# The MLP of three batches in 64-row mode, two PSUM tiles at a time with swapped row halves

## The chip, the cores and the metric

The kernel runs on one core of a Trainium2 chip (trn2). The metric is the device time of one execution in microseconds. Each run is repeated, and the runs of two kernels that are compared alternate on the same chip. A profile is of one execution; its span is some 2 us shorter than the device time.

Names used below: PE is the TensorE matmul engine, PEld its weight loads, DVE is VectorE, ACT is ScalarE, POOL is GpSimd. `psc` are scores in PSUM, `est` their exponentials, `pav` the values in PSUM, `pa` and `ph` the two low-rank mixing products, `pt` the first MLP product and `pch` the second. The instructions that empty these PSUM tiles are named by what they write: `xs` (the scaled values, with the 16-bit copy `xh`), `a` (from `pa`), `xf` (`xs` plus `ph`; its transposed copy is `uT`), `tT` (the relu of `pt`) and `of` (the output, from `pch`). `pturn` are transposes of q and k on PE.

## The reference, cut to what matters

```python
# block-sparse attention over 4 batches x 8 heads, 768 x 64 each
scores = scale * np.matmul(q, k.transpose(0, 1, 3, 2))       # masked by 32 x 32 blocks
attn = np.exp(scores - max); attn = attn / attn.sum(-1)
x = np.matmul(attn, v)                                        # -> (4, 768, 512)
# low-rank mixing over the sequence, then an MLP 512 -> 2048 -> 512
h = x.transpose(0, 2, 1) @ U @ V                              # rank 32
u = x + h.transpose(0, 2, 1)
out = u + np.maximum(u @ w_ch1, 0.0) @ w_ch2
```

## The kernel before

Attention works by head pairs (16 in all, four per batch) and by *units*: one exp over a 128x1024 tile of scores, nine units per pair. The MLP of a batch runs as a "fill" between the scores of the next batch. PSUM has eight banks (the Trainium skill, "PSUM — Partial Sum Buffer", Specifications (TRN2)), and the kernel allots them all: four hold two score tiles, and everything else (`pav`, `pa`, `ph`, `pt`, `pch`) shares the other four, chosen by a small clock model at build time. From the second batch on, the scores of each head contract over 64 rows only, so the matmuls of a pair's two heads lie on different row halves and run side by side; the MLP contracts over 128 rows.

```python
    banks = [0.0] * 4                       # when each of the four banks comes free, by the model
    def pst_tile(shape, dtype, name, tag=None):
        if tag is None:
            n = min(range(4), key=lambda n: banks[n])
            clk["pe"] = max(clk["pe"], banks[n])
        ...                                 # cut
    def scores(i, u, est):
        ...                                 # cut
            for h in range(2):              # two matmuls, row halves 0 and 1, two banks
                    mm(o, kT[rows[h], kc], qT[rows[h], q0:q1], True, True)
        keep(nc.scalar.activation(out=est, in_=psc, func=AF.Exp, scale=0.125))

    def mlp_steps(b):
        def w1(jj, c):                      # one pt tile: 4 matmuls of 128 rows x 384 columns
            pt = pst_tile([P, HS], FP32, "pt")
            for cc in range(NCC):
                mm(pt, w1t[:, cc, jj * P : (jj + 1) * P],
                   uT[:, cc, c * HS : (c + 1) * HS], cc == 0, cc == NCC - 1, us=0.162)
            ...                             # relu on ACT or DVE, whichever the model says is first
        def w2(sc, part, n0=0, n1=HD):      # one pch tile: 16 matmuls of 128 rows x 512 columns
            ...                             # cut

    groups = [[x] for x in stream[:SINGLE]]                       # SINGLE = 8
    groups += [stream[n : n + 2] for n in range(SINGLE, len(stream), 2)]
    while gi < len(groups) or work or beside:
        for i, u in groups[gi] if gi < len(groups) else []:
            scores(i, u, est)               # two units per group
        while beside and beside[0][0] <= gi: beside.popleft()[1]()   # second mixing step
        ...                                 # masks on DVE, loads
        if fill: run_fill(sum(c for c, _ in fill) / (to_come[0] - gi))  # MLP steps
        while work and work[0][0] <= gi: work.popleft()[1]()         # values, first mixing step
        gi += 1
```

The softmax here doesn't subtract the row's maximum and nothing guards it: scores larger than these inputs give would overflow.

Of the kernel before, what the change touches and what calls it, by code (L numbers as in the profile page):

```python
# [17 lines left out]
P = 128  # L18
# [3 lines left out]
def kernel(  # L22
# [84 lines left out]
    def pst_tile(shape, dtype, name, tag=None):  # L107
        if tag is None:
            n = min(range(4), key=lambda n: banks[n])
            clk["pe"] = max(clk["pe"], banks[n])  # L110
        else:
            n = pairs[tag][0]
            pairs[tag].rotate(1)
        t = psp.tile(shape, dtype, tag=f"bank{n}", name=name)
        banks[n] = OPEN
        held[id(t)] = (n, t)
        return t
# [8 lines left out]
    def mm(out, lhsT, rhs, start, stop, loose=False, us=0.0):  # L126
        clk["pe"] += us
        keep(
            nc.tensor.matmul(  # L129
                out, lhsT, rhs, start=start, stop=stop, skip_group_check=loose  # L130
            )
        )

# [85 lines left out]
    keep(nc.vector.memset(Vd, 0.0))  # L219
# [138 lines left out]
    mvld = w2t[0:R, 0:3, :].rearrange("r j d -> r (j d)").bitcast(FP32)  # L358
# [123 lines left out]
    def values(i, c, ests, xs, xh):  # L482
        b, hp = divmod(i, HP)
        pav = new_pav()
        for h in range(2):
            for j in range(3):
                for g in range(T):
                    mm(
                        pav[:, j, h, :],
                        weights(ests, g, 3 * c + j, h),  # L490
                        vts[b % 2][:, 2 * hp + h, g, 0 : D + 1],
                        g == 0, g == T - 1, us=0.0315,
                    )
        norm(i, c, pav, xs, xh)

    def mix_a(i, xh, box, part, tag=None):
        if part == 0:
            box["pa"] = pst_tile([P, P], FP32, "pa", tag)
        for sc in range(3 * part, 3 * part + 3):
            mm(box["pa"], Ut[:, sc, :], xh[:, sc, :], sc == 0, sc == T - 1, us=0.056)  # L500
        if part == 1:
            box["a"] = misc.tile([P, P], FP16, tag="a16", name="a16")
            keep(nc.vector.tensor_copy(out=box["a"], in_=box["pa"]))
            give_back(box["pa"], run_on("dve", 0.2))

# [62 lines left out]
    def mlp_steps(b):  # L568
# [3 lines left out]
        def w1(jj, c):  # L572
# [11 lines left out]
            dst = tT[jj][:, c * HS : (c + 1) * HS]  # L584
            ends = {e: max(clk[e], clk["pe"]) + d for e, d in (("act", 0.43), ("dve", 0.48))}
            if ends["act"] <= ends["dve"]:
                keep(nc.scalar.activation(out=dst, in_=pt, func=AF.Relu))  # L587
                give_back(pt, run_on("act", 0.43))
            else:
                keep(nc.vector.tensor_scalar_max(out=dst, in0=pt, scalar1=0.0))  # L590
                give_back(pt, run_on("dve", 0.48))
# [3 lines left out]
        def w2(sc, part, n0=0, n1=HD):  # L595
# [9 lines left out]
            if part == 3:  # L605
                of = opool.tile([P, n1 - n0], FP32, tag="of", name="of")
                keep(
                    nc.vector.tensor_add(out=of, in0=xfs[b][:, sc, n0:n1], in1=pchs[sc])  # L608
                )
                give_back(pchs[sc], run_on("dve", 0.6))  # L610
                keep(
                    nc.sync.dma_start(
                        out=out[b].rearrange("(p t) d -> p t d", t=T)[:, sc, n0:n1],
                        in_=of,
                    )
                )

        for jj in range(NJJ):
            for c in range(2):
                steps.append((0.65, lambda jj=jj, c=c: w1(jj, c)))  # L620
        for sc in range(T):
            cuts = [(0, HD)] if (b, sc) != (B - 1, T - 1) else [(0, 384), (384, HD)]
            for n0, n1 in cuts:
                for part in range(4):
# [3 lines left out]
                            lambda sc=sc, part=part, n0=n0, n1=n1: w2(sc, part, n0, n1),  # L628
                        )
# [46 lines left out]
    def turn_part(i, nm, part):  # L676

        if part == 0:
            turning[nm] = pst_tile([P, T, P], FP16, "pturn", tag="ps")
# [23 lines left out]
    def at_unit(i, u):  # L703
        if (i, u) in MASKS:
            mask_tiles(MASKS.index((i, u)))
        if i == 0:
# [16 lines left out]
            if u == 1:  # L723
# [8 lines left out]
                keep(nc.sync.dma_start(out=mvld, in_=moe_V))  # L732
# [17 lines left out]
        if u == 0:  # L750
            issue(i + 3)
            if i == 1:
                for h in range(2):
                    keep(
                        nc.gpsimd.tensor_copy(
                            out=Ut[:, :, h * D : h * D + R],
                            in_=uld.rearrange("p (t r) -> p t r", t=T),
                        )
                    )
                keep(  # L760
                    nc.gpsimd.tensor_copy(
                        out=Vt[0:R, :, :],
# [3 lines left out]
        if i == 2 and u == 0:  # L766
            for h in range(2):
                keep(nc.sync.dma_start(out=Vd[h * D : h * D + R], in_=Vt[0:R]))
# [29 lines left out]
    def run_fill(us):  # L798
        state["debt"] += us
        while fill and state["debt"] > 0:  # L800
            cost, fn = fill.popleft()
            fn()
            state["debt"] -= cost
# [3 lines left out]
    def pair_tail(i, ests, xs, xh):  # L807
# [3 lines left out]
        def both_a():  # L811
            mix_a(i, xh, box, 0)
            mix_a(i, xh, box, 1)

        def both_h():
# [4 lines left out]
            lambda: values(i, 0, ests, xs, xh),  # L820
            lambda: values(i, 1, ests, xs, xh),
            both_a,
# [5 lines left out]
    groups = [[x] for x in stream[:SINGLE]]  # L828
    groups += [stream[n : n + 2] for n in range(SINGLE, len(stream), 2)]
    LATE = 8  # L830
    OPENS = [5]
    for b in range(1, B):
        last = [n for n, gr in enumerate(groups) if (HP * b + HP - 1, NU - 1) in gr][0]
        OPENS.append(last + 1 + LATE)
# [8 lines left out]
    while gi < len(groups) or work or beside:  # L843
# [13 lines left out]
        for _ in range(len(unmasked) if gi >= SINGLE else 2 if gi > OPENS[0] else 0):  # L857
            i, u, est = unmasked.popleft()
            mask_mul(u, est)
            if u == NU - 1:  # L860
                steps = pair_tail(i, *live.pop(i))
                for at, fn in zip((0, 1, 3), steps):
                    work.append((gi + at, fn))
                beside.append((gi + 5, steps[3]))
# [35 lines left out]
        if fill:  # L900
            to_come = [n for n in OPENS if n > gi] or [gi + 1]
            run_fill(sum(c for c, _ in fill) / (to_come[0] - gi))
# [42 lines left out]
```

## Time and profile before

| | before |
|---|---|
| time, median of the runs | 290.8 us (3 runs), later 290.1 to 290.6 |
| span of the profiled run, clock | 288.9 us, 0.999 |
| PE busy | 279.8 us, 97% |
| prologue, up to the first `pt` matmul | 50.0 us |
| middle, to the start of the last batch's MLP | 194.4 us |
| last batch's MLP, alone, with the closing steps of the program | 44.5 us |

The head of the page of before: span, busy time by engine with its share and instruction count, and PE's row of the 40 equal slices of the span (a digit is the busy share in tenths, 9 is 90% or more).

```profile
span 288.9 us, 6744 instructions
...
PE 279.8 (97%) x2765; PEld 162.0 (56%) x2765; DVE 188.3 (65%) x347; ACT 178.0 (62%) x232; POOL 95.3 (33%) x126
...
PE   7979998899999999999999999999999999999996
```

The chain of work that ended last, by engine and then by line, as shares of the span (the page of before, part 4). L129 is the line of the helper through which nearly all matmuls go, so the names tell them apart:

```profile
PE 84%; DMA 6%; ACT 6%; issue 2%; DVE 1%; POOL 1%; SPq 0%; ACTq 0%; DVEq 0%; POOLq 0%
PE pt L129 29%; PE pch L129 29%; PE psc L129 11%; PE pav L129 10%; ACT est L419 5%; DMA ka<-onehot_const 3%; DMA qld<-in_q_dram 2%; PE pa L129 2%; DMA kld<-in_k_dram 1%; PE ph L129 1%; PE pturn L194 0%; PE puT L563 0%; DVE uT L564 0%; DVE xh L453 0%; DVE m L384 0%
```

And the list of PE's waits of before in the middle, 50 to 244.4 us (who waited for whom, total us, times, longest):

```profile
engine line waited for: us in total, times, longest us
PE pturn L194 <- ACT tT L587: 0.6, 1, 0.6
PE psc L129 <- ACT est L419: 0.5, 1, 0.5
PE pt L129 <- DVE uT L564: 0.2, 1, 0.2
```

PE bounds the middle: it waits 1.3 us in 194. But "busy" is not "at full rate". The Trainium skill says in "Trainium Kernel Development and Optimization", Performance Expectations, that matmul busy time is a bad metric because matmuls are pipelined. It is so here: a 512-column matmul is shown as 380 ns long and the next one starts 216 ns after it. The timeline of PE in before (start, length, form, count):

```profile
137.70 0.49 PE L129 MATMUL pt<-uT,w1t 128*128 128x384 f16 x2
138.12 0.61 PE L129 MATMUL psc<-qT,kT 64*128 64x512 f16 x4
138.66 2.12 PE L129 MATMUL pt<-uT,w1t 128*128 128x384 f16 x12
```

Four score matmuls of 64 rows are two side-by-side pairs of 216 ns, 0.43 us; from 138.12 to 138.66 they take 0.54. The 0.1 us is the change from 64-row to 128-row mode.

**How the ledgers below are made.** From the trace I took the start of every matmul. Two 64-row matmuls of one kind that run side by side count as one. From each start-to-start time I took off the streaming time, as the trace shows it inside long runs (32 ns for 65 columns, 56 for 128, 109 for 256, 162 for 384, 216 for 512). What remains is excess. It is sorted by place: at a change between 64-row and 128-row matmuls 96 ns are booked as mode change; at a swap (known from program order) what is above 40 ns is booked as swap; the rest above 40 ns is booked on what ended just before, and what is below 40 ns is "small". For the middle of before: streaming 180.7 us, mode changes 108 x 96 ns = 10.4 us, waits 2.2 us, small remains 1.0 us; together, but for rounding, the 194.4 us.

### The profile page before, as it was taken

The numbers are of one execution on the slowest core, as the hardware profiler recorded it, in microseconds if no ns is written. First come the engines' busy times: TensorE is split into PE (matmuls) and PEld (weight loads), VectorE is DVE, ScalarE is ACT, GpSimd is POOL, SyncE is SP. The second block draws the span as 40 slices with busy tenths as digits, with TensorE's granted clock in tenths as the row PEclk, the third lists the DMA queues.
The fourth block names the chain that finished last, engine by engine and source line by source line (L and its number), as shares of the span: only waits on it lengthen the run. The fifth ranks groups of instructions, "written<-read, shape, count | busy, mean of one in ns | idle before, by whom it ended". The sixth has DMA issues, their size and how long they took to land.

```text
span 288.9 us, 6744 instructions
## 1 busy us (share of the span) xinstructions
PE 279.8 (97%) x2765; PEld 162.0 (56%) x2765; DVE 188.3 (65%) x347; ACT 178.0 (62%) x232; POOL 95.3 (33%) x126
## 2 busy tenths in 40 slices
PE   7979998899999999999999999999999999999996
PEld 2557775455746454556565545466564644665443
DVE  5756768689997978887886695779787622000112
ACT  3879999687785757577776555577875000776000
POOL 1549853207344454526244261603031201000000
PEclk9999999999999999999999999999999999999999
DMA  5999999962457677773444365161010225000122
GB/s 157 331 261 262 236 254 268 243 169 76 92 140 107 213 160 205 202 153 64 144 108 142 106 173 143 50 93 31 0 31 0 58 80 102 36 0 2 70 75 74
DMA packets 46414, 36.91 MB, mean 128 GB/s; under 512 B 27272, under 2 KB 42896, under 8 KB 46384
## 3 DMA queue, kind: packets, MB, share of 16 engines
q1 hardware_dynamic: 43208, 32.06, 41.6%
q0 software_dynamic: 2688, 4.19, 8.1%
q8 instruction: 21, 0.34, 0.5%
q10 hardware_dynamic: 488, 0.24, 0.3%
q14 instruction: 9, 0.07, 0.1%
HBM read 27.80 MB, written 6.29 MB: 118 GB/s over the span
## 4 chain that ended last, share of the span: by engine, by line
PE 84%; DMA 6%; ACT 6%; issue 2%; DVE 1%; POOL 1%; SPq 0%; ACTq 0%; DVEq 0%; POOLq 0%
PE pt L129 29%; PE pch L129 29%; PE psc L129 11%; PE pav L129 10%; ACT est L419 5%; DMA ka<-onehot_const 3%; DMA qld<-in_q_dram 2%; PE pa L129 2%; DMA kld<-in_k_dram 1%; PE ph L129 1%; PE pturn L194 0%; PE puT L563 0%; DVE uT L564 0%; DVE xh L453 0%; DVE m L384 0%
## 5 line engine op out<-in xcount | busy, mean ns | idle before, releaser
L419 ACT ACTIVATE est<-psc 128x1024 f16<-128x1024 f32 x144 | 138.8, 1023 | 47.4 <-PE psc L129 47.2
L129 PE MATMUL pt<-uT,w1t 128*128 128x384 f16 x512 | 89.1, 327 | 0.2 <-DVE uT L564 0.2
L129 PE MATMUL pch<-w2t,tT 128*128 128x512 f16 (+2 forms) x400 | 87.9, 371 | 0.0
L431 DVE TENSOR_TENSOR est<-est,m 128x1024 f16<-128x1024 f16 x108 | 84.7, 828 | 0.0
L129 PEld LDWEIGHTS <-w1t 128*128 128x128 f16 x512 | 47.6, 98 | 38.2 <-issue 8.4
L587 ACT ACTIVATE tT<-pt 128x384 f16<-128x384 f32 x82 | 39.3, 495 | 36.1 <-PE pt L129 34.9
L129 PEld LDWEIGHTS <-tT 128*128 128x128 f16 x400 | 36.4, 98 | 44.3 <-issue 5.4
L129 PEld LDWEIGHTS <-est 128*128 128x128 f16 x1152 | 44.0, 97 | 10.6 <-issue 0.5
L471 POOL CAST xh<-xs 128x384 f16<-128x384 f32 x30 | 21.4, 716 | 84.7 <-DVE xs L453 82.5
L608 DVE TENSOR_TENSOR of<-xf,pch 128x512 f32<-128x512 f32 (+2 forms) x25 | 16.6, 662 | 49.9 <-PE pch L129 49.8
L129 PE MATMUL pav<-vt,est 128*128 128x65 f16 x1152 | 46.4, 193 | 0.1
L129 PE MATMUL psc<-qT,kT 64*128 64x512 f16 (+1 forms) x288 | 33.9, 327 | 0.9 <-ACT est L419 0.8
L549 POOL CAST uh<-xf 128x384 f16<-128x384 f32 x24 | 16.1, 697 | 38.3 <-issue 33.6
L590 DVE TENSOR_SCALAR tT<-pt 128x384 f16<-128x384 f32 x46 | 24.2, 548 | 0.9 <-PE pt L129 0.7
L129 PE MATMUL psc<-qa,ka 128*128 128x512 f16 (+1 forms) x96 | 21.8, 326 | 1.9 <-DMA ka<-onehot_const 1.5
L448 DVE RECIPROCAL rcp<-pav 128x6 f32<-128x6 f32 x32 | 6.2, 194 | 21.1 <-PE pav L129 20.6
L453 DVE TENSOR_TENSOR xs<-pav,rcp 128x384 f32<-128x384 f32 x32 | 17.8, 557 | 1.9
L188 POOL CAST kst<-kld 128x768 f16<-128x768 f32 x15 | 16.5, 1100 | 5.5 <-PE pt L129 2.0
L188 POOL CAST qst<-qld 128x768 f16<-128x768 f32 x15 | 16.5, 1100 | 3.6 <-PE pa L129 2.5
L129 PEld LDWEIGHTS <-kT 64*128 64x128 f16 x288 | 10.1, 94 | 13.4 <-issue 8.8
L182 POOL CAST vt<-vld 128x768 f16<-128x768 f32 x16 | 15.0, 939 | 5.7 <-DMA vld<-in_v_dram 5.7
L544 DVE TENSOR_TENSOR xf<-xs,ph 128x384 f32<-128x384 f32 x24 | 12.2, 548 | 4.5 <-PE ph L129 4.5
(57 smaller groups left out, 111.5 us busy)
## 6 DMA issues: line engine op xcount, KB each, us to landing
vld<-in_v_dram SPq DMA_DIRECT2D x16, 384.0 KB, 5.0
out_dram<-of SPq DMA_DIRECT2D x23, 256.0 KB, 2.2
qld<-in_q_dram SPq DMA_DIRECT2D x15, 384.0 KB, 4.4
kld<-in_k_dram SPq DMA_DIRECT2D x15, 384.0 KB, 4.1
w1t<-in_moe_w_ch_dram POOLq DMA_DIRECT2D x4, 512.0 KB, 10.2
w2t<-in_moe_w_ch_dram POOLq DMA_DIRECT2D x4, 512.0 KB, 19.5
qld<-in_q_dram SPq DMA_DIRECT2D x1, 256.0 KB, 3.1
kld<-in_k_dram SPq DMA_DIRECT2D x1, 256.0 KB, 4.5
```

The lines of the kernel that those rows point to most:

```text
L129: nc.tensor.matmul(out, lhsT, rhs, start=start, stop=stop, skip_group_check=loose)
L182: nc.gpsimd.tensor_copy(out=vts[b % 2][:, 2 * hp : 2 * hp + 2, :, 0:D], in_=ld)
L188: keep(nc.gpsimd.tensor_copy(out=st.rearrange("p t h d -> p h t d"), in_=ld))
L419: keep(nc.scalar.activation(out=est, in_=psc, func=AF.Exp, scale=0.125))
L431: keep(nc.vector.tensor_tensor(out=o, in0=o, in1=m, op=ALU.mult))
L453: nc.vector.tensor_tensor(out=o.rearrange("p j (h d) -> p j h d", h=2), in0=pav[:, :, :, 0:D], in1=rcp[:, :, :, None].broadcast_to([P, 3, ...
L471: keep(nc.gpsimd.tensor_copy(out=xh[:, 3 * c : 3 * c + 3, :], in_=x3))
L544: nc.vector.tensor_tensor(out=u3, in0=xs[:, tc3, :], in1=phs[c], op=ALU.add)
L549: keep(nc.gpsimd.tensor_copy(out=uh[:, tc3, :], in_=u3))
L587: keep(nc.scalar.activation(out=dst, in_=pt, func=AF.Relu))
L590: keep(nc.vector.tensor_scalar_max(out=dst, in0=pt, scalar1=0.0))
L608: nc.vector.tensor_add(out=of, in0=xfs[b][:, sc, n0:n1], in1=pchs[sc])
```

## The change

The intent is to take away most of the 108 mode changes: if the MLP and the mixing products run in 64-row mode too, they can follow the scores with no drain. Each 128-row matmul becomes two 64-row matmuls on the two row halves. The Trainium skill ("TensorEngine Tiling (Array Packing)", Gotcha 1: PSUM Pressure) says that different row tiles cannot use one PSUM bank at the same time. So two tiles are made at once: in the first half of the work row half 0 adds to tile 0 and row half 1 to tile 1, then they swap. Between the two halves the kernel makes PE wait until its own last matmul has left the array, because the other row half now writes that bank; the scores of one unit are placed there to cover the wait. Values stay in 128-row mode, both halves of a pair in one burst. The last batch, which has no scores to cover swaps, stays in 128-row mode.

The core of the diff (cut; comments are mine):

```diff
+    def half_wait(ins):                       # PE waits for its own earlier matmul
+        nop = nc.tensor.nop(nofuse=True)
+        tc.add_manual_dep(nop.ins, ins.ins.name, ...)
+        keep(nop)
...
-    def values(i, c, ests, xs, xh):
+    def values(i, ests, xs, xh):              # both halves, c = 0 and 1, in one burst
...
+    def mix_a_rows(xh, box):                  # pa in two banks, one per row half, summed on DVE
+        pas = [pst_tile([P, P], FP32, "pa") for r in range(2)]
...
+        def w1_rows(jj, phase):
+            if phase == 0:
+                pair[0] = [pst_tile([P, HS], FP32, "pt") for c in range(2)]
+            pts = pair[0]
+            if phase == 1:
+                half_wait(pair[2])
+            for cc in range(NCC):
+                for r in ((0, 1), (1, 0))[phase]:
+                    c = r ^ phase
+                    last = mm(pts[c], w1t[rows[r], cc, jj * P : (jj + 1) * P],
+                        uT[rows[r], cc, c * HS : (c + 1) * HS],
+                        phase == 0 and cc == 0, phase == 1 and cc == NCC - 1, True, us=0.081)
+            if phase == 0:
+                pair[2] = half_done(last)
+            else:
+                for c in range(2):
+                    relu(tT[jj][:, c * HS : (c + 1) * HS], pts[c])
...                                            # w2_rows likewise, 16 pairs per half
     def run_fill(us):
         state["debt"] += us
+        n = 0
         while fill and state["debt"] > 0:
+            if fill[0][2] and n and us < 1e6:  # a second half waits for the next scores
+                break
...
-    groups = [[x] for x in stream[:SINGLE]]
-    groups += [stream[n : n + 2] for n in range(SINGLE, len(stream), 2)]
+    groups = [[x] for x in stream]            # one unit per group
...
-                for at, fn in zip((0, 1, 3), steps):
-                    work.append((gi + at, fn))
-                beside.append((gi + 5, steps[3]))
+                work.append((gi, steps[0]))
+                work.append((gi + 5, steps[1]))
+                beside.append((gi + 9, steps[2]))
...                                            # in the prologue: V loaded twice (mvld), U copied
-                            out=Ut[:, :, h * D : h * D + R],      # in 4 pieces of 64 rows, not 2
+                                out=Ut[rows[r], :, at : at + R],
```

More of the change, by code (lines that the diff above doesn't have):

```diff
@@ L109, in pst_tile @@
             n = min(range(4), key=lambda n: banks[n])
+            assert banks[n] < OPEN
             clk["pe"] = max(clk["pe"], banks[n])
@@ L127, in mm, with half_done @@
         clk["pe"] += us
-        keep(
-            nc.tensor.matmul(
-                out, lhsT, rhs, start=start, stop=stop, skip_group_check=loose
-            )
-        )
+        ins = nc.tensor.matmul(
+            out, lhsT, rhs, start=start, stop=stop, skip_group_check=loose
+        )
+        keep(ins)
+        return ins
+    def half_done(ins):
+        return ins
+    def half_wait(ins):
+        nop = nc.tensor.nop(nofuse=True)
+        tc.add_manual_dep(
+            nop.ins, ins.ins.name,
+            mybir.DependencyInfo(mybir.DependencyClass.Sync, mybir.DependencyReason.DATA),
+            reason="halves",
+        )
+        keep(nop)
     id16 = consts.tile([P, P], FP16)
@@ L218 @@
     keep(nc.vector.memset(Vt, 0.0))
-    keep(nc.vector.memset(Vd, 0.0))
     qld, kld = new_ld(0, "q"), new_ld(0, "k")
@@ L357 @@
     uld = w2t[:, 3, 0 : 2 * T * R].bitcast(FP32)
-    mvld = w2t[0:R, 0:3, :].rearrange("r j d -> r (j d)").bitcast(FP32)
+    mvld = w2t[0 : 2 * R, 0:3, :].rearrange("r j d -> r (j d)").bitcast(FP32)
     def load_w1(cc):
@@ L480, in new_pav @@
         return pst_tile([P, 3, 2, D + 1], FP32, "pav", tag)
-    def values(i, c, ests, xs, xh):
+    def values(i, ests, xs, xh):
         b, hp = divmod(i, HP)
-        pav = new_pav()
-        for h in range(2):
-            for j in range(3):
-                for g in range(T):
-                    mm(
-                        pav[:, j, h, :],
-                        weights(ests, g, 3 * c + j, h),
-                        vts[b % 2][:, 2 * hp + h, g, 0 : D + 1],
-                        g == 0, g == T - 1, us=0.0315,
-                    )
-        norm(i, c, pav, xs, xh)
+        for c in range(2):
+            pav = new_pav()
+            for h in range(2):
+                for j in range(3):
+                    for g in range(T):
+                        mm(
+                            pav[:, j, h, :],
+                            weights(ests, g, 3 * c + j, h),
+                            vts[b % 2][:, 2 * hp + h, g, 0 : D + 1],
+                            g == 0, g == T - 1, us=0.0315,
+                        )
+            norm(i, c, pav, xs, xh)
     def mix_a(i, xh, box, part, tag=None):
@@ L504, in mix_a @@
             give_back(box["pa"], run_on("dve", 0.2))
+    def mix_a_rows(xh, box):
+        pas = [pst_tile([P, P], FP32, "pa") for r in range(2)]
+        for sc in range(T):
+            for r in range(2):
+                mm(pas[r], Ut[rows[r], sc, :], xh[rows[r], sc, :], sc == 0, sc == T - 1, us=0.027)
+        a16 = box["a"] = misc.tile([P, P], FP16, tag="a16", name="a16")
+        keep(nc.vector.tensor_copy(out=a16, in_=pas[0]))
+        give_back(pas[0], run_on("dve", 0.2))
+        keep(nc.vector.tensor_tensor(out=a16, in0=a16, in1=pas[1], op=ALU.add))
+        give_back(pas[1], run_on("dve", 0.2))
     def mix_h(i, c, a16, xs, uh, tag=None, quick=False):
@@ L583, in w1 @@
                 )
-            dst = tT[jj][:, c * HS : (c + 1) * HS]
-            ends = {e: max(clk[e], clk["pe"]) + d for e, d in (("act", 0.43), ("dve", 0.48))}
-            if ends["act"] <= ends["dve"]:
-                keep(nc.scalar.activation(out=dst, in_=pt, func=AF.Relu))
-                give_back(pt, run_on("act", 0.43))
-            else:
-                keep(nc.vector.tensor_scalar_max(out=dst, in0=pt, scalar1=0.0))
-                give_back(pt, run_on("dve", 0.48))
+            relu(tT[jj][:, c * HS : (c + 1) * HS], pt)
         pchs = {}
@@ L605, in w2 @@
             if part == 3:
-                of = opool.tile([P, n1 - n0], FP32, tag="of", name="of")
-                keep(
-                    nc.vector.tensor_add(out=of, in0=xfs[b][:, sc, n0:n1], in1=pchs[sc])
-                )
-                give_back(pchs[sc], run_on("dve", 0.6))
-                keep(
-                    nc.sync.dma_start(
-                        out=out[b].rearrange("(p t) d -> p t d", t=T)[:, sc, n0:n1],
-                        in_=of,
-                    )
-                )
+                leave(sc, n0, n1, pchs[sc])
@@ new lines, in mlp_steps, with relu @@
+        pair = {}
+        def relu(dst, pt):
+            ends = {e: max(clk[e], clk["pe"]) + d for e, d in (("act", 0.43), ("dve", 0.48))}
+            if ends["act"] <= ends["dve"]:
+                keep(nc.scalar.activation(out=dst, in_=pt, func=AF.Relu))
+                give_back(pt, run_on("act", 0.43))
+            else:
+                keep(nc.vector.tensor_scalar_max(out=dst, in0=pt, scalar1=0.0))
+                give_back(pt, run_on("dve", 0.48))
+        def w1_rows(jj, phase):
+            if phase == 0:
+                tT[jj] = tpool.tile([P, S], FP16, tag="tT", name="tT")
+                pair[0] = [pst_tile([P, HS], FP32, "pt") for c in range(2)]
+            uT = uTs[b].rearrange("p n t s -> p n (t s)")
+            pts = pair[0]
[4 more added lines that the diff above has]
+                    c = r ^ phase
+                    last = mm(
+                        pts[c],
+                        w1t[rows[r], cc, jj * P : (jj + 1) * P],
+                        uT[rows[r], cc, c * HS : (c + 1) * HS],
+                        phase == 0 and cc == 0, phase == 1 and cc == NCC - 1, True,
+                        us=0.081,
+                    )
+            if phase == 0:
+                pair[2] = half_done(last)
+            else:
+                for c in range(2):
+                    relu(tT[jj][:, c * HS : (c + 1) * HS], pts[c])
@@ new lines, in leave, with w2_rows @@
+        def leave(sc, n0, n1, pch):
+            of = opool.tile([P, n1 - n0], FP32, tag="of", name="of")
+            keep(nc.vector.tensor_add(out=of, in0=xfs[b][:, sc, n0:n1], in1=pch))
+            give_back(pch, run_on("dve", 0.6))
+            keep(
+                nc.sync.dma_start(
+                    out=out[b].rearrange("(p t) d -> p t d", t=T)[:, sc, n0:n1],
+                    in_=of,
+                )
+            )
+        def w2_rows(s0, phase, part):
+            if phase == 0 and part == 0:
+                pair[1] = [pst_tile([P, HD], FP32, "pch") for c in range(2)]
+            if phase == 1 and part == 0:
+                half_wait(pair[2])
+            for jj in range(4 * part, 4 * part + 4):
+                for r in ((0, 1), (1, 0))[phase]:
+                    c = r ^ phase
+                    last = mm(
+                        pair[1][c],
+                        tT[jj][rows[r], (s0 + c) * P : (s0 + c + 1) * P],
+                        w2t[rows[r], jj, :],
+                        phase == 0 and jj == 0, phase == 1 and jj == NJJ - 1, True,
+                        us=0.1085,
+                    )
+            if phase == 0 and part == 3:
+                pair[2] = half_done(last)
+            if phase == 1 and part == 3:
+                for c in range(2):
+                    leave(s0 + c, 0, HD, pair[1][c])
@@ new lines, in mlp_steps @@
+        if b < B - 1:
+            for jj in range(NJJ):
+                for phase in range(2):
+                    steps.append((0.65, lambda jj=jj, ph=phase: w1_rows(jj, ph), phase == 1))
+            for s0 in range(0, T, 2):
+                for phase in range(2):
+                    for part in range(4):
+                        steps.append(
+                            (
+                                0.87,
+                                lambda s0=s0, ph=phase, part=part: w2_rows(s0, ph, part),
+                                phase == 1 and part == 0,
+                            )
+                        )
+            return steps
@@ L618, in mlp_steps @@
         for jj in range(NJJ):
             for c in range(2):
-                steps.append((0.65, lambda jj=jj, c=c: w1(jj, c)))
+                steps.append((0.65, lambda jj=jj, c=c: w1(jj, c), False))
         for sc in range(T):
@@ L628, in mlp_steps @@
                             lambda sc=sc, part=part, n0=n0, n1=n1: w2(sc, part, n0, n1),
+                            False,
                         )
@@ L678, in turn_part @@
         if part == 0:
-            turning[nm] = pst_tile([P, T, P], FP16, "pturn", tag="ps")
+            turning[nm] = pst_tile([P, T, P], FP16, "pturn", tag="ps" if i < HP + 1 else None)
         turn_some(sts[i, nm], turning[nm], 3 * part, 3 * part + 3)
@@ L731, in at_unit @@
                 issue(2, "v")
-                keep(nc.sync.dma_start(out=mvld, in_=moe_V))
+                for h in range(2):
+                    keep(nc.sync.dma_start(out=mvld[h * R : h * R + R], in_=moe_V))
                 keep(
@@ L753, in at_unit @@
                 for h in range(2):
-                    keep(
-                        nc.gpsimd.tensor_copy(
-                            out=Ut[:, :, h * D : h * D + R],
-                            in_=uld.rearrange("p (t r) -> p t r", t=T),
+                    for r in range(2):
+                        at = h * D + r * R
+                        keep(
+                            nc.gpsimd.tensor_copy(
+                                out=Ut[rows[r], :, at : at + R],
+                                in_=uld[rows[r]].rearrange("p (t r) -> p t r", t=T),
+                            )
                         )
-                    )
                 keep(
                     nc.gpsimd.tensor_copy(
-                        out=Vt[0:R, :, :],
+                        out=Vt[0 : 2 * R, :, :],
                         in_=mvld.rearrange("r (p t) -> r t p", t=T),
@@ L767, in at_unit @@
             for h in range(2):
-                keep(nc.sync.dma_start(out=Vd[h * D : h * D + R], in_=Vt[0:R]))
+                keep(nc.sync.dma_start(out=Vd[rows[h]], in_=Vt[rows[0]]))
         if (i, u) in WLOADS:
@@ L799, in run_fill @@
         state["debt"] += us
+        n = 0
         while fill and state["debt"] > 0:
-            cost, fn = fill.popleft()
+            if fill[0][2] and n and us < 1e6:
+                break
+            cost, fn, _ = fill.popleft()
             fn()
+            n += 1
             state["debt"] -= cost
@@ L809, in pair_tail @@
         uh = xpool.tile([P, T, P], FP16, tag="uh", name="uh")
-        def both_a():
-            mix_a(i, xh, box, 0)
-            mix_a(i, xh, box, 1)
         def both_h():
@@ L819, in pair_tail @@
         return [
-            lambda: values(i, 0, ests, xs, xh),
-            lambda: values(i, 1, ests, xs, xh),
-            both_a,
+            lambda: values(i, ests, xs, xh),
+            lambda: mix_a_rows(xh, box),
             both_h,
@@ L827 @@
     SINGLE = 8
-    groups = [[x] for x in stream[:SINGLE]]
-    groups += [stream[n : n + 2] for n in range(SINGLE, len(stream), 2)]
-    LATE = 8
+    groups = [[x] for x in stream]
+    LATE = 16
     OPENS = [5]
@@ L833 @@
         last = [n for n, gr in enumerate(groups) if (HP * b + HP - 1, NU - 1) in gr][0]
-        OPENS.append(last + 1 + LATE)
+        OPENS.append(last + LATE)
     for name in ("pe", "dve"):
@@ L901 @@
             to_come = [n for n in OPENS if n > gi] or [gi + 1]
-            run_fill(sum(c for c, _ in fill) / (to_come[0] - gi))
+            run_fill(sum(c for c, _, _ in fill) / (to_come[0] - gi))
         while work and work[0][0] <= gi:
```

## The prediction

> **What bounds the kernel now.** TensorE (PE). The page has PE busy 279.8 of 288.9 us (97%), DVE 188.3, ACT 178.0; the clock is 0.999. The chain of waits is 84% PE (MLP matmuls pt 29% and pch 29%, scores 11%, values 10%). The list of waits for 60 to 230 us shows PE itself waiting 0.5 us. So only PE issue time counts.
>
> **What is lost.** From starts of neighbouring matmuls in the trace: in a run of one kind they follow at streaming rate: 162 ns (384 columns), 216 (512), 32 (65). Two 64-row matmuls on different row halves start 3 to 4 ns apart and the pair takes one streaming time (about 216 ns for 512 columns, 109 for 256). Each change between 128-row and 64-row matmuls adds time, in both directions: 512 to scores 312 instead of 216, 384 to scores 258 instead of 162, values to scores 126 instead of 30, scores to pt 308 instead of 216: about 94 ns, and the second issue after it is about 10 ns late. The Trainium skill, "TensorEngine Tiling (Array Packing)", Key Properties, says that changing the tiling mode drains TensorE; this trace agrees, with about 104 ns per change. Between 50 and 244 us there are about 108 changes, so about 11 us.
>
> **What the change does.**
> - Removes: MLP, scores and both mixing steps of batches 0 to 2 share the 64-row mode. Left are two changes per head pair (one values burst) for 12 pairs and a few at the start, about 30. About 78 go: -8 us (7 to 9), all on the PE chain.
> - Streaming is unchanged: twice the matmuls, at half the cost each as pairs, weight loads hidden.
> - Adds 57 swaps (48 in pt, 9 in pch), each a PE wait for its own last matmul. A reader of PSUM starts about 200 ns after a matmul's streaming ends, and a PE semaphore instruction takes 51 ns. One score unit covers only 216 ns. I estimate 50 to 130 ns left per uncovered swap, and some 0.3 us for two or three in the tail, where no scores are left: +4 us (2 to 7).
> - Adds PSUM pressure: two of four banks stay open. During pt the other pair is being emptied (relu 495 ns on ACT, 548 on DVE, queued behind a 1023 ns exp or a 677 to 990 ns mask), while values, pa or ph want it, and the next pair wants both banks at once. I estimate 0.1 to 0.8 us at each of about 18 such places: +4 us (1 to 8).
>
> **Predicted:** 288.5 us, range 283 to 296. Faster by over 2%: 0.28; within 2%: 0.60; slower: 0.12. Mode changes alone would give about 282.5.
>
> **What in the profile would show each step.**
> - Mode changes: about 30 after 50 us, with the 94 ns unchanged at those left.
> - Streaming: a 384-column pair every 162 ns, a 512-column pair every 216. If pairs take longer, weight loads are not hidden.
> - Swaps: the gap from the score pair to the first matmul of the second half is its 216 ns plus 50 to 130.
> - Banks: PE waits released by ACT tT, DVE tT, DVE xs or DVE xf, at values, pa and the following pt; together 1 to 8 us, against 0.5 before.
>
> **What would make it wrong.** Swaps fully hidden and banks free in time: 283 or below. If relu falls behind (ACT and DVE are each 70 to 90% busy in the pt stages, by the windows view) bank waits repeat in every pt group: above 296. If a pair's stream is slowed, by 10 ns each for 670 pairs, that is 7 us.

## The result, and the profile after

| | before | after |
|---|---|---|
| time, median | 290.6 us (4 runs) | 299.72 us (299.32 to 301.79, 4 runs) |
| ratio | | 1.0326 (1.0274 to 1.0378): slower |
| span of the profiled run, clock | 288.9 us, 0.999 | 298.2 us, 0.994 |
| prologue | 50.0 us | 51.7 us |
| middle | 194.4 us | 201.3 us |
| last MLP and closing steps | 44.5 us | 45.3 us |

The clock is not the reason: the run of after at clock 1.0 took 299.4 us. The head of the page of after, its chain of work by engine, and PE's waits of after in the middle (51.7 to 252.9 us):

```profile
span 298.2 us, 8304 instructions
...
PE 283.3 (95%) x3509; PEld 175.7 (59%) x3509; DVE 186.0 (62%) x352; ACT 182.7 (61%) x238; POOL 94.4 (32%) x128
...
PE   7979998999999999899999999999999989999995
...
PE 74%; DVE 10%; ACT 8%; DMA 4%; issue 2%; ACTq 0%; POOL 0%; SPq 0%; DVEq 0%
PE pch L129 27%; PE pt L129 23%; PE pav L129 11%; PE psc L129 9%; ACT est L433 7%; DVE est L445 4%; DMA ka<-onehot_const 3%; PE pa L129 2%; DVE tT L638 1%; DVE of L667 1%; DMA w1t<-small_const 1%; DVE xf L571 1%; PE ph L129 1%; PE pturn L209 1%; PE warm L129 0%
```

```profile
engine line waited for: us in total, times, longest us
PE pch L129 <- DVE of L667: 1.5, 4, 0.6
PE pt L129 <- DVE of L667: 1.3, 4, 0.5
PE pa L129 <- DVE tT L638: 1.1, 3, 0.5
PE pav L129 <- DVE est L445: 0.4, 1, 0.4
PE pt L129 <- DVE uT L591: 0.4, 1, 0.4
PE pt L129 <- DVE tT L638: 0.3, 1, 0.3
PE ph L129 <- DVE tT L638: 0.2, 1, 0.2
```

In before the chain was PE almost alone after the start; now DVE has 10% of it: 4% is the mask multiplication `est`, and `tT`, `of` and `xf`, which empty PSUM tiles, have 1% each. In the list, 4.4 of the 5.2 us are waits for `of` and `tT`. The list shows 5.2 us against 1.3, and a reader would stop there; but PE's busy time *rose*, as modelled ends hide the first 160 ns of each wait. The ledger shows the whole, in us:

```
middle            length  streaming  mode changes  swaps  wait for mask  banks, other  small
before             194.4      180.7   108: 10.4      -        -             2.2         1.0
after              201.3      180.7    27:  2.6     5.7      1.1           10.7         0.5
```

So the mode changes did go. Streaming is booked at the same rates in both, so its equal sums test nothing; the starts do: in after the median pair of `pt` takes 162 ns and of `pch` 216, against 163 and 216 for one matmul in before. 64-row pairs run at full rate. The 7.8 us gained were paid back twice over: 5.7 us at swaps, 8.5 us more at banks, and 1.1 us where values waited for a mask. How these look in the timeline of after. A swap, with the same pair of scores once after the wait is long over (because `pa` came in between) and once right after a first half:

```profile
141.20 0.44 PE L129 MATMUL pa<-xh,Ut 64*128 64x128 f16 x9
141.44 0.41 PE L129 MATMUL psc<-qT,kT 64*128 64x512 f16 x2
141.66 1.53 PE L129 MATMUL pt<-uT,w1t 64*128 64x384 f16 x16
142.96 0.44 PE L129 MATMUL psc<-qT,kT 64*128 64x512 f16 x2
143.33 0.50 PE L129 MATMUL pt<-uT,w1t 64*128 64x384 f16 x4
```

At 141.44 the pair takes 0.22 us to the next `pt`; at 142.96 it takes 0.37. (Most swaps behind scores lose 0.12 us, this one 0.16.) A bank wait, all engines:

```profile
146.26 0.40 PE L129 MATMUL psc<-qT,kT 64*128 64x512 f16 x2
...
146.50 0.35 PE L129 MATMUL ph<-a,Vd 64*128 64x128 f16 x6
...
146.67 2.08 PE L129 MATMUL pt<-uT,w1t 64*128 64x384 f16 x16
...
146.87 1.02 DVE L571 TENSOR_TENSOR xf<-xs,ph 128x384 f32<-128x384 f32 x2 [0.49 <-PE ph L129]
147.47 0.09 PEld L129 LDWEIGHTS <-w1t 64*128 64x128 f16 x1 [0.22 <-issue]
...
147.94 0.42 PEld L129 LDWEIGHTS <-w1t 64*128 64x128 f16 x6 [0.37 <-issue]
```

`ph` takes the two banks that are not held by the open `pt` pair, and DVE empties them one after the other from 146.87 to 147.89. The second half of the open pair is done at 147.3, and the next pair wants both banks. Its first matmul starts at 147.47, when the first `xf` is done; its partner on the other row half starts only at 147.94, when the second one is. In the timeline PE is busy without a break for all 16 matmuls, yet eight pairs should stream in 1.30 us and these lose 0.46 us at this one place. While one half waits for its bank, the other half does not go on. The start of each later `pt` stage is worse: from 124.5 us of after PE loses 1.1 us while DVE empties the two `pch` tiles of the batch before:

```profile
124.53 0.40 PE L129 MATMUL psc<-qT,kT 64*128 64x512 f16 x2
124.70 1.27 DVE L667 TENSOR_TENSOR of<-xf,pch 128x512 f32<-128x512 f32 x2
125.42 0.32 PE L129 MATMUL pt<-uT,w1t 64*128 64x384 f16 x1 [0.49 <-DVE of L667]
126.02 0.81 PE L129 MATMUL pt<-uT,w1t 64*128 64x384 f16 x7 [0.28 <-DVE of L667]
```

The Trainium skill has the general warning, in "TensorEngine Tiling (Array Packing)", Performance Considerations, PSUM Bottleneck: tiling speeds up TensorE but not the emptying of PSUM. Here nothing was sped up, but two tiles now complete in the same moment, and the same holds.

The prologue is 1.7 us longer. (In this profile the clock was 0.95 over the first 20 us, against 1.00 in before, which may be part of it; the comparison of all profiles under i_pro is the better measure.) POOL in after, 20 to 25 us; before had two copies of `Ut` at 20.50 to 21.14 and `xh` at 22.60:

```profile
21.08 1.50 POOL L854 CAST Ut<-w2t 64x192 f16<-64x192 f32 x4 [0.17 <-DMA w2t<-in_moe_U_dram]
22.64 1.57 POOL L860 CAST Vt<-w2t 64x768 f16<-64x768 f32 x1
24.16 0.95 POOL L485 CAST xh<-xs 128x384 f16<-128x384 f32 x2
```

Four copies of 64 rows take 1.50 us where two of 128 rows took 0.64, and U lands later (at 21.0 us against 20.3) behind the two loads of V. `xh`, which the first `pa` needs, comes 1.6 us later. I had taken this part of the diff for nothing. The last 0.8 us lie after the last MLP: its matmuls take the same time in both, but from the last `of` to the end of the program after takes 3.24 us and before 2.49.

### The profile page after: what moved, and what is told of

It reads as the page before. It is cut to its first block, busy times and chain, and to the rows that moved or that the text cites. A ratio compares the mean times of both kernels' runs of the same rounds, so it can differ in the third digit from the quotient of the medians.

```text
span 298.2 us, 8304 instructions
## 1 busy us (share of the span) xinstructions
PE 283.3 (95%) x3509; PEld 175.7 (59%) x3509; DVE 186.0 (62%) x352; ACT 182.7 (61%) x238; POOL 94.4 (32%) x128
## 4 chain that ended last, share of the span: by engine, by line
PE 74%; DVE 10%; ACT 8%; DMA 4%; issue 2%; ACTq 0%; POOL 0%; SPq 0%; DVEq 0%
PE pch L129 27%; PE pt L129 23%; PE pav L129 11%; PE psc L129 9%; ACT est L433 7%; DVE est L445 4%; DMA ka<-onehot_const 3%; PE pa L129 2%; DVE tT L638 1%; DVE of L667 1%; DMA w1t<-small_const 1%; DVE xf L571 1%; PE ph L129 1%; PE pturn L209 1%; PE warm L129 0%
## 5 line engine op out<-in xcount | busy, mean ns | idle before, releaser
L433 ACT ACTIVATE est<-psc 128x1024 f16<-128x1024 f32 x144 | 144.1, 1027 | 59.4 <-PE psc L129 57.2
L129 PE MATMUL pt<-uT,w1t 64*128 64x384 f16 (+1 forms) x896 | 97.5, 323 | 2.6 <-DVE of L667 1.3
L129 PE MATMUL pch<-w2t,tT 64*128 64x512 f16 (+3 forms) x688 | 92.6, 372 | 1.6 <-DVE of L667 1.5
L445 DVE TENSOR_TENSOR est<-est,m 128x1024 f16<-128x1024 f16 x108 | 82.2, 772 | 7.8 <-ACT est L433 7.6
L129 PEld LDWEIGHTS <-w1t 64*128 64x128 f16 (+1 forms) x896 | 53.4, 94 | 37.9 <-issue 14.3
L129 PEld LDWEIGHTS <-tT 64*128 64x128 f16 (+1 forms) x688 | 41.5, 95 | 38.7 <-issue 4.3
L635 ACT ACTIVATE tT<-pt 128x384 f16<-128x384 f32 x88 | 42.5, 494 | 28.0 <-PE pt L129 26.3
L129 PE MATMUL pav<-vt,est 128*128 128x65 f16 x1152 | 45.3, 194 | 0.7 <-DVE est L445 0.4
L129 PE MATMUL psc<-qT,kT 64*128 64x512 f16 (+1 forms) x288 | 43.6, 324 | 0.3 <-ACT est L433 0.3
L638 DVE TENSOR_SCALAR tT<-pt 128x384 f16<-128x384 f32 x40 | 22.1, 553 | 5.1 <-PE pt L129 4.8
L129 PEld LDWEIGHTS <-kT 64*128 64x128 f16 x288 | 16.7, 94 | 9.4 <-issue 0.6
```

The source lines that it names most:

```text
L129: ins = nc.tensor.matmul(out, lhsT, rhs, start=start, stop=stop, skip_group_check=loose)
L445: keep(nc.vector.tensor_tensor(out=o, in0=o, in1=m, op=ALU.mult))
L635: keep(nc.scalar.activation(out=dst, in_=pt, func=AF.Relu))
L638: keep(nc.vector.tensor_scalar_max(out=dst, in0=pt, scalar1=0.0))
```

## The experiments

**The theory** after reading the trace: the loss is swaps (5.7 us; the first ledger, which is quoted in the expectations, had 4.9, because it missed a few in `pch`) and PSUM banks (about 10 us): two of four banks stay open, and the other two are being emptied when `pav`, `pa`, `ph` or the next pair want them. **Rivals**: the swaps alone do it, directly or by what they delay; or the new grouping (one unit per group, bursts) does it; or DVE is overloaded, so that evictions queue.

Ten kernels ran. The ledger of all ten beside before and after, in us, is here for reference; "prologue" is the time to the first `pt`, and differs by 1 to 2 us from run to run:

```
                 median  ratio   prologue  middle  mode changes  swaps  wait for mask  banks, other  small
before           290.6             50.0    194.4    108: 10.4      -        -             2.2         1.0
after            299.72  1.0326    51.7    201.3     27:  2.6     5.7      1.1           10.7         0.5
a_noswap         297.28  1.0238    52.0    199.6     27:  2.6     0        1.1           14.8         0.4
b_fuse           298.60  1.0270    51.8    199.9     27:  2.6     1.6      1.1           12.7         1.2
d_order          296.15  1.0186    51.2    197.5     27:  2.6     6.3      2.3            5.1         0.5
e_both           293.53  1.0110    51.2    195.1     27:  2.6     1.9      2.4            6.3         1.3
c_mlp128         302.80  1.0428    50.8    205.0    210: 20.2      -       0.1            1.9         2.1
f_nomask         299.06  1.0293    53.2    199.6     27:  2.6     5.7      0              9.9         0.6
h_before_nomask  290.76  1.0026    49.3    194.5    108: 10.4      -        -             2.4         1.0
g_later          292.51  1.0079    52.8    193.7     27:  2.6     2.0      0.8            6.1         1.6
i_pro            290.66  0.9998    50.4    193.7     27:  2.6     2.0      0.8            6.1         1.6
j_tail           289.15  0.9955    49.6    192.9     31:  3.0     1.3      0.8            5.5         1.6
```

The interval of after's own ratio (1.0274 to 1.0378) is 3 us wide, so a difference of 1 or 2 us to after does not stand on the times alone. The length of the middle does better: g_later and i_pro, whose edits differ only in how U and V are loaded, agree there to 0.02 us.

### a_noswap: no swap at all (wrong result)

```diff
-            if phase == 1:
-                half_wait(pair[2])
...
-                    c = r ^ phase
+                    c = r                    # each row half stays on its tile; likewise in w2_rows
```

> Wrong result on purpose: in the second half of a pt or pch pair each row half stays on its own PSUM tile, so no swap and no PE wait for its own matmul; everything else is as after. Theory (ledger of PE starts: swaps cost 4.9 us, 110 ns each at 45 uncovered ones, PSUM bank waits about 11 us): -4 to -6 us against 299.7, so about 295, still slower than before; bank waits stay. Rival 1 (the swaps are the main loss, directly or by what they delay): back to 291 or below. Rival 2 (scores unit by unit, bursts, other grouping): no change to speak of.

Measured: 297.28 us, 2.4 us less than after; 1.0238 (1.0202 to 1.0274). In the middle it is 1.6 us less. Less than the theory's lower end, and far from rival 1. The ledger tells why: all 5.7 us of swaps went, and 4.1 us came back at banks (14.8 against 10.7). In PE's list of waits, which hides part of each, `pa` behind `tT` grew from 1.1 to 2.1 us and `ph` behind `tT` from 0.2 to 0.4. My reading: the swap's wait had been giving ACT and DVE time to empty tiles. Swaps are not the main loss, and the two losses are not independent.

### b_fuse: the wait without its own instruction

```diff
-        nop = nc.tensor.nop(nofuse=True)
+        nop = nc.tensor.nop(nofuse=False)    # the wait goes to the first instruction of the second half
```

> Same waits, right result, but the wait is carried by the first instruction of the second half and not by a separate PE semaphore instruction. Theory (the bubble is the 51 ns semaphore instruction plus 56 ns until a load and a matmul start again, since the awaited matmul ends about when the covering scores do): bubbles fall from 107 to 20 to 50 ns, -2.5 to -4.5 us, about 296. Rival (the bubble is the time until the awaited matmul has ended): no change, 299.7.

Measured: 298.6 us, 1.1 us less than after (1.3 in the middle); correct. The bubble at the 42 `pt` swaps behind scores fell from 110 to 35 ns on average (the typical one from 120 to 15), as expected, so most of it was the separate semaphore instruction: the trace of after shows it 51 ns long, the load 76 ns and the matmul 107 ns after its start. But 2.0 of the 4.1 us came back at banks. The mechanism held, the size did not, as in a_noswap.

### d_order: other places for the same bank requests

```diff
-                work.append((gi + 5, steps[1]))
-                beside.append((gi + 9, steps[2]))
+                beside.append((gi + 5, steps[1], False))   # first mixing step after the scores
+                beside.append((gi + 9, steps[2], True))    # its group opens no new pair
...
+            if hold and fill[0][3]:            # this step would take two new banks
+                return n
...
+            n = run_fill(us, hold=hold or due)
+            while work and work[0][0] <= gi:   # values, before a new pair is opened
+                work.popleft()[1]()
+            if due and not hold:
+                run_fill(0.0, n=n)
```

> Same work and same swaps as after, right result; only the places change where PSUM banks are taken: in a group with values, the new pt pair is opened after the values, not before; the first mixing step runs after the scores, not after the fill; and no new pair is opened in the group of the second mixing step. Theory (PE waits about 11 us for banks because two of four stay open and the other two are being emptied): bank waits fall to about half, -4 to -7 us, about 294. Rivals (swaps alone, or grouping): within 1 us of 299.7.

Measured: 296.15 us, 3.6 us less than after; correct; 1.0186 (1.0159 to 1.0213). Bank waits fell to about half, 10.7 to 5.1 us, with the same work, swaps and mode changes; 1.2 us came back as values waiting for their mask (they are now 0.65 us earlier) and 0.6 at swaps. PE's waits of d_order in the middle (51 to 248.5 us) show it:

```profile
engine line waited for: us in total, times, longest us
PE pav L129 <- DVE est L445: 1.8, 3, 0.7
PE pch L129 <- DVE of L667: 0.8, 2, 0.6
PE pt L129 <- DVE uT L591: 0.4, 1, 0.4
PE pav L129 <- DVE of L667: 0.4, 1, 0.4
PE pa L129 <- DVE tT L638: 0.2, 1, 0.2
PE pch L129 <- PE pch L129: 0.2, 1, 0.2
```

The waits of `pt` behind `of` and `tT` are gone from the list, and that of `pa` behind `tT` is 0.2 us, from 1.1. This is the direct test of the bank theory, and it held; the two rivals said no change.

### e_both: b_fuse and d_order together

The edit is the sum of the two.

> b_fuse and d_order together. Theory: the gains add, -7 to -11 us against 299.7, so 289 to 293, about level with before (290.6). Rival (one wait hides behind the other): no more than the better of the two.

Measured: 293.53 us, 6.2 us less than after; 1.0110 (1.0086 to 1.0134). The theory's range, 7 to 11 us, was missed by 0.8. The two gains do not hide behind each other: 6.2 us is more than 1.1 + 3.6. Once banks are free in time, a shorter swap is worth more (4.4 us of swaps went against d_order, 1.2 came back at banks).

### c_mlp128: the MLP back in 128-row mode

```diff
-        if b < B - 1:
+        if False:
             for jj in range(NJJ):
                 for phase in range(2):
                     steps.append((0.65, lambda jj=jj, ph=phase: w1_rows(jj, ph), phase == 1))
```

> One part undone: the MLP of batches 0 to 2 is back in 128-row mode; scores unit by unit, the value burst and the 64-row mixing stay. Right result. Mode theory (96 to 105 ns per change, both ways): every single-unit group with MLP work now has two changes, about 200 after the first 50 us against 27, so about +17 us of mode changes, while swaps (4.9 us) and most bank waits (about 10 us) go: 300 to 304 us. If changes of mode cost nothing: about 284. If the grouping (unit by unit, burst) is itself the loss: well above 304.

Measured: 302.8 us; 1.0428 (1.0399 to 1.0457); correct. There are 210 mode changes in the middle, and the ledger has nothing else of size: 20.2 us of mode changes and 1.9 us of waits. Against before, 102 more changes and a middle that is 10.6 us longer: 104 ns each, small remains included. PE of c_mlp128 in the timeline:

```profile
139.92 1.47 PE L129 MATMUL pt<-uT,w1t 128*128 128x384 f16 x8
141.33 0.39 PE L129 MATMUL psc<-qT,kT 64*128 64x512 f16 x2
141.65 1.47 PE L129 MATMUL pt<-uT,w1t 128*128 128x384 f16 x8
```

Eight `pt` matmuls stream in 1.30 us and take 1.41; a pair of scores streams in 0.22 and takes 0.32. So the premise of the change is right, and the grouping costs nothing but its own mode changes: that rival falls.

### f_nomask and h_before_nomask: is DVE too busy? (wrong results on purpose)

```diff
-        keep(nc.vector.tensor_tensor(out=o, in0=o, in1=m, op=ALU.mult))
-        run_on("dve", 0.6, ready[id(est)])
```

> Wrong result on purpose: after without the 108 mask multiplications on DVE (82 us of DVE time). Theory (PE waits for banks because relu, xs, xf and of queue behind other work on DVE and ACT, not because of the eviction's own length): bank waits fall from about 10 us to 3 to 5, so -4 to -7 us, about 294; swaps stay at about 4.9 us. Rival (the waits are set by the order of the PE program and the length of one eviction): within 1.5 us of 299.7.

> Control, wrong result on purpose: before without the same mask multiplications. Before has under 1 us of waits for DVE or ACT in its middle, so all theories: within 1.5 us of 290.5. If it falls by as much as f_nomask does, then f_nomask shows nothing about banks.

Measured: f_nomask 299.06 us (1.0293), h_before_nomask 290.76 us (1.0026, the control). The edit does a little more than it says: the model that chooses the engine of each relu at build time now counts DVE as free, so 14 of the 128 relus moved from ACT to DVE (54 there, from 40), and DVE's busy time fell by 68 us (186.0 to 118.0), not by the 82 of the masks. With that, the bank waits of after fell only from 10.7 to 9.9 us; the 1.1 us of values waiting for masks went, and the prologue of this profile happened to be 1.5 us longer. My theory's part "evictions queue behind masks" fell; the rival, order of the PE program and length of an eviction, is the one that agrees. Whether evictions that queue behind an exp on ACT matter as much was not tried.

### g_later: values one group later, V copied later

```diff
-                work.append((gi, steps[0]))
+                work.append((gi + 1, steps[0]))
...
-                keep(nc.gpsimd.tensor_copy(out=Vt[0 : 2 * R, :, :], ...))   # at pair 1, unit 0
+                keep(nc.gpsimd.tensor_copy(out=Vt[0 : 2 * R, :, :], ...))   # at pair 1, unit 3
```

> e_both, with the values one group later (they waited 2.35 us for masks in e_both) and the GpSimd copy of V after the first xh cast instead of ahead of it (the prologue is 1 to 2 us longer in every kernel with the change, with PE pa waiting for POOL xh). Right result. Theory: -2 us of value waits and -1 us of prologue against 293.5: 290 to 291.5, level with before. Beats before by over 1 us only if waits do not come back elsewhere.

Measured: 292.51 us, 1.0 us less than e_both; 1.0079 (1.0045 to 1.0113); correct. The value waits fell from 2.4 to 0.8 us. The prologue did not get shorter (52.8 us; U landed at 22.2 us in this profile, 1.2 later than in after): PE's `pa` still waited for `xh`, and `ph` now waited 0.5 us for V. Half of this expectation missed.

### i_pro: U and V loaded as before

```diff
-                for h in range(2):
-                    keep(nc.sync.dma_start(out=mvld[h * R : h * R + R], in_=moe_V))
+                keep(nc.sync.dma_start(out=mvld, in_=moe_V))
...                                            # and Ut in two copies of 128 rows, Vt after them
```

> g_later with U and V loaded and copied as in before (one V load, two copies of U, V after them; the sum of the two pa tiles is the same). Right result. Theory (the extra V load and four instead of two U copies hold up GpSimd, whose xh cast PE waits for): the time to the first pt matmul goes back from 51 to 53 us to about 50, so -1 to -2 us against 292.5: 290.5 to 291.5. Rival (the prologue differs by chance from run to run): no change, 292.5.

Measured over 5 rounds: 290.66 us; 0.9998 (0.9978 to 1.0017); correct. The prologue took 50.4 us, and the time fell by 1.9 us against g_later (another set of runs of before: their ratios differ by 0.008, which is 2.3 us). Over all profiles, the eight with the changed loading have a prologue of 50.8 to 53.2 us (mean 51.8) and the four with the old one 49.3 to 50.4 (mean 49.8). They also differ at the very end: from the last `of` to the end of the program, 3.21 to 3.25 us in the eight and 2.48 to 2.51 in the four. Which part of the loading does that was not looked for. So this side part of the diff cost 2 us in the prologue and 0.7 at the end.

### j_tail: no swaps where no scores are left

```diff
-            for s0 in range(0, T, 2):
+            for s0 in range(0, T if b < B - 2 else 2, 2):
...
+            if b == B - 2:                     # last four output tiles of batch 2 in 128-row mode
+                for sc in range(2, T):
+                    for part in range(4):
+                        steps.append((0.87, lambda sc=sc, part=part: w2(sc, part), False, part == 0))
```

> i_pro, with the last four output tiles of batch 2 in 128-row mode, because most of them run after the last scores, where a swap has nothing to hide behind. Right result. Theory: some 2 us of waits (pch for its own half and for DVE of) go and at most 4 changes of mode come (0.4 us): -0.5 to -1.5 us against i_pro, 289 to 291, level with before or better by under 0.5%. Rival (these waits come back as others, as in a_noswap): within 0.5 us of i_pro.

Measured over 5 rounds: 289.15 us; 0.9955 (0.9930 to 0.9980); correct. It is 1.5 us faster than i_pro on the same chip, at the edge of what was expected, of which 0.8 us are in the middle by the ledger (swaps -0.7, banks -0.6, mode changes +0.4) and the rest in the prologue of the profiled run, where the two programs are the same, so that part is chance. It beats before by 0.45%, with an interval that leaves out 1, and after by 10.6 us.

## Why the prediction was wrong

The time was 299.72 us, above the range of 283 to 296, and the direction was wrong.

- **Bounded by PE, mode changes.** Right. Predicted about 108 before, about 30 after, -8 us; measured 108, 27 and -7.8 (at the 96 ns that the ledger books). c_mlp128 shows the same price from the other side. The Trainium skill's "Mode switching requires drain" ("TensorEngine Tiling (Array Packing)", Key Properties) agrees with all of it, without a number; this case gives 96 ns, and 104 with the slower second issue.
- **Streaming unchanged.** Right: by the starts a pair takes 162 ns (384 columns) and 216 ns (512). No pair was slowed.
- **Swaps.** Right in kind and nearly in size: predicted +4 us (2 to 7), measured 5.7; 110 ns at each of 42 `pt` swaps behind scores, where I had said 50 to 130, and 0.5 us at the one bare swap of the tail. What a swap is worth when taken away is another matter: 5.7 us of swaps gone saved 2.4 us of time and 1.6 in the middle (a_noswap).
- **PSUM banks: the step that failed.** The prediction put it as "I estimate 0.1 to 0.8 us at each of about 18 such places: +4 us (1 to 8)". The kind of wait was right and most of the places; the term was mis-sized. Measured: waits for banks and other producers 10.7 us against 2.2 before, so +8.5, and +1.1 for values waiting for masks, which I had not listed. I counted values, `pa` and `ph`, but not the openings of `pt` and `pch` stages (1.1 us at 124.5 us alone; in a recount by the tile that waits, `pt` has 5.4 us of the 11.8, `pa` and `pch` 2.3 each, values 1.0, `ph` 0.7), nor that a pair whose second bank is late holds up both row halves. The reason I gave, evictions queued behind masks, is refuted for the masks on DVE by f_nomask. d_order shows the cause of 5.6 us of it: the order in which PE asks for banks.
- **The sign that I missed.** "PE waits released by ACT tT, DVE tT, DVE xs or DVE xf" was half right: of the four only `tT` on DVE is in the list, the trace at 147 us shows `xf`, and `of`, the largest, was missing. "Together 1 to 8 us" is what the list of waits shows (5.2), and it is too low: PE's modelled ends hide about half.
- **The prologue and the closing steps.** Not in the prediction. About +2 us and +0.7, shown by i_pro.
- **My own sum.** The terms that I wrote add up to -8 + 4 + 4 = 0, so 290.8 us; the 288.5 took off 2.3 us for which the text has no term. With the measured terms, -7.8 + 5.7 + 8.5 + 1.1 and -0.5 of small remains make +7.0 us for the middle (201.3 - 194.4 = 6.9), and in the profiles the prologue adds 1.7 and the end 0.8.

What stays open: the 5.5 us of bank waits that are left in j_tail were not taken apart, nor was ACT's share in them. That the banks could not be given more room was not tested: all eight are in use.

## What to carry to other kernels

A change that makes two PSUM tiles complete in the same moment needs two free banks in that moment, so count, at each place where PE asks for a bank, how long ago its last user ended and how long emptying takes; this costs more here (8.5 us) than the 81 drains that the change removed (7.8 us). Waits on a full engine trade places: taking one away gave half to 70% of it back elsewhere here, until the next limit, the order of bank requests, was mended too. Judge a saturated PE by the starts of its matmuls, not by busy shares or lists of waits, and cost the small side edits of a diff as well.

## What the Trainium skill lacked or had wrong

- "TensorEngine Tiling (Array Packing)", Key Properties, says that a change of tiling mode drains TensorE, but not what that costs: 96 ns per change here, in both directions and for all widths from 65 to 512 columns, and the second issue after it some 10 ns late.
- "TensorEngine Tiling (Array Packing)", Gotcha 1: PSUM Pressure says that different row tiles cannot use one bank at once and that software must synchronise. It does not give the price of handing a bank from one row tile to the other on PE itself: about 110 ns behind a 216 ns pair of scores with a separate semaphore instruction (51 ns, next matmul 107 ns after its start), about 35 ns with the wait on the next instruction, some 0.5 us with nothing in between.
- No page that I read says that a row tile whose bank is late holds up the other row tile: at 147.47 us of after, a pair that should take 162 ns took 468, as its second matmul started 463 ns after the first. It follows from "TensorE: Matmul & The Clock Gate", Part 3 (matmuls are strictly first in, first out), with which it agrees.
- "Trainium Kernel Development and Optimization" calls matmul busy time a bad metric, and weight-load busy share and flop rate good ones. Here the weight-load share misled as well: it rose from 56% to 59% in the slower kernel, because 64-row mode loads twice as many pieces. Of the measures tried, only the starts of the matmuls showed the loss; the flop rate was not worked out.
